# Dilated attention tiles ahead of the plain ones, and the first batch's low-rank product in fp32, in a fused attention and FFN kernel on Trainium2

## The chip, the core and the metric

The kernel runs on one core of one Trainium2 chip. A core has five engines that are named here as the profile names them: PE (TensorE, the matrix products; PEld is its weight load), DVE (VectorE), ACT (ScalarE), POOL (GpSimd) and SP (SyncE, which here does nothing but issue DMA transfers, one after the other). Each engine works through its own instructions in a fixed order and waits on semaphores for the others. The metric is the device time of one execution in microseconds (us).

## What is computed

```python
def _attn_ref(q, k, v):                       # 8 batches, 8 heads, S=576, D=64
    scores = scale * np.matmul(q, k.transpose(0, 1, 3, 2))
    rel = pos[:, None] - pos[None, :]
    mask_plain = (rel >= 0) & (rel < window)                     # window 32, heads 0 to 3
    mask_dil = (rel >= 0) & (rel < window * dilation) & (rel % dilation == 0)   # dilation 4, heads 4 to 7
    ...                                                          # masked softmax
    return np.matmul(attn, v)

def _moe_ref(x, U, V, w_ch1, w_ch2):          # x: 8 x 576 x 512 from the attention
    h = x.transpose(0, 2, 1) @ U @ V          # U: 576 x 32, V: 32 x 576, mixes along the sequence
    u = x + h.transpose(0, 2, 1)
    ch = np.maximum(u @ w_ch1, 0.0) @ w_ch2   # 512 -> 2048 -> 512
    return u + ch
```

## The kernel before

**Layout.** The 8 x 576 tokens are 36 tiles of 128 tokens, `x_tile(t)`, 512 wide: columns 0 to 255 hold the four plain heads (half 0), 256 to 511 the dilated ones (half 1). The FFN goes over 12 chunks of three tiles (384 tokens). In a chunk 16 blocks `f` run: `layer1(f)` (L760 on) makes `ph` out of `u` transposed and the columns of `w_ch1` (products at L771), ACT applies the relu (`hh`, L776), DVE makes the rest `hl` (L777), and `layer2(f)` adds three products per tile into `acc` (L791). FFN operands are split into a high and a low part in the type fp32r, with three products each: high times high, high times low, low times high.

**Attention.** A batch is nine groups `g` of two tiles of 64 queries (`TILES`, L49, sets which). Scores (L389 for the first two batches, in fp32), softmax (DVE L409, ACT L413), transposes of the weights (PE L426, copied as `pt` at L428 and L430), products with `v` (`weighted`, PE L452), and an eviction that divides by the sum (DVE L482, four operations per group). A plain tile is evicted straight into its rows of `x`. A dilated tile holds every fourth token, is evicted to `xp`, and SP then moves it row by row with DMAs `x<-xp` (L486) to where its tokens stand. Batch 0 is a prologue; batch 1 is laid over chunk 0, and every later batch over the chunks that follow.

**The mix.** `t` is U times x, per batch in two column halves, `t_0` (plain) and `t_1` (dilated). `split` (L494 on) splits a piece of x into `xhl` (ACT cast L500, subtraction L502), `t_mm` (L509 on) adds two fp32r products per piece (L522), and `t_evict` (L527 on) splits `t` once more into `ts` (ACT L531 and L537, DVE L532 and L534). `mix` adds V times t to x (PE `m`, L546, DVE L548). The three tiles of chunk 0 do it otherwise: `lay_x` (L556) transposes x by products with the identity, `lay_mix` (L563) adds the mix to the transposed tile, `transp` (L604, L605) splits that into `uth` and `utl`, and `add_mix` (L569) puts the mix into `acc`.

**Weights.** The two weight matrices arrive as 32 pieces of 64-bit words, `raw` (512 KB, SP L202 and L204). `weight_step` runs a pipeline over the pieces: ACT narrows in three operations (`narrow_a`, L211 to L213), DVE shifts (L219), POOL adds (L220), then the high part is a cast on ACT (L224) or DVE (L226) and the low part a subtraction on POOL or DVE (L227). Pieces alternate: `w1(f)`, `w2(f)`. All 32 are prepared between the end of the prologue and the end of chunk 0. The first three small pieces are U and V.

**What sets the order.** A scheduler of the framework turns the program into a fixed order per engine: by priorities, by the order in which the program issues, and by its own estimates. The program steers it with tables at its head: after which step of batch 0 a weight step stands (`PRE_AT`, `W_FROM`, `W_EACH`, `PRE_N`), and which engine takes a cast (`H_ON_ACT`, `XL_DVE`, `XL_LAST`). `batch_items` (L608 on) lists the pieces of a batch in order, with a place in time for each.

## Time and profile before

| | |
|---|---|
| median of three runs | 1012.73 us (1011.54 to 1014.42) |
| the profiled execution, time | 1013.52 us |
| its span | 1011.7 us |
| mean granted clock of PE | 0.982 |
| busy: PE, PEld, DVE, ACT, POOL | 984.7, 864.9, 626.8, 408.6, 328.3 us |
| chain that ended last, by engine | PE 89%, DVE 4%, DMA 2%, POOL 1%, ACT 1%, issue 1% |
| largest groups of PE | layer 2 `acc` (three groups, 576 each) 229.3, 228.0, 212.0 us; layer 1 `ph` (three groups, 768 each) 175.5, 174.3, 173.2 us |

The span is the time from the first to the last instruction that the profiler saw; the time of the execution has some us around it. The chain follows the work that ended last backwards, at each step to what released it. An engine's idle time means something only where the chain runs through it. SPq rows are SP's issues of transfers: the second number of such a row is how long the issues of that group took, not how long the transfers took.

### The profile page before, as it was taken

To read this page: it belongs to the slowest core of one execution; us is meant where nothing else is said; L and a number is where in the kernel's file an instruction comes from. 1 tells how busy PE (TensorE), PEld (TensorE's weight loads), DVE (VectorE), ACT (ScalarE), POOL (GpSimd) and SP (SyncE) were. 2 spreads that over 40 slices of the span, in tenths; PEclk is the share of its full clock that TensorE was granted. 3 is DMA by queue.
4 is the path that set the end of the run, shared out by engine and by line. 5 is a ranking of instruction groups with operands and counts; after the bars stand their busy time and mean duration, and the time that the engine had idled before them with its cause. 6 is when DMAs were issued, how large, how long until landed. Compare 5 with 4: busy or idle time off the path is not lost.

```text
span 1011.7 us, 18252 instructions
## 1 busy us (share of the span) xinstructions
PE 984.7 (97%) x5928; PEld 864.9 (85%) x5928; DVE 626.8 (62%) x2149; ACT 408.6 (40%) x985; POOL 328.3 (32%) x520
## 2 busy tenths in 40 slices
PE   7699999999999999999999999999999999999998
PEld 6598778888988889888888888788898888899996
DVE  4989877776468747777468763877647864311211
ACT  5799954343244424344244432434324432111110
POOL 0579954252133413153132431434222421000000
PEclk9789997999999999999999999999999999999999
DMA  9688634342333325243242332424232420400000
GB/s 291 186 276 270 183 120 110 81 129 85 75 88 112 86 59 140 77 120 83 66 124 73 114 83 73 122 77 124 85 88 80 119 64 22 135 1 1 32 1 32
DMA packets 96912, 103.34 MB, mean 102 GB/s; under 512 B 12816, under 2 KB 83536, under 8 KB 96816
## 3 DMA queue, kind: packets, MB, share of 16 engines
q1 hardware_dynamic: 96816, 102.16, 35.6%
q8 instruction: 48, 0.79, 0.3%
q14 instruction: 48, 0.39, 0.1%
...
## 4 chain that ended last, share of the span: by engine, by line
PE 89%; DVE 4%; DMA 2%; POOL 1%; ACT 1%; issue 1%; SPq 0%; DVEq 0%; POOLq 0%
PE ph L771 38%; PE acc L791 38%; PE pv L452 4%; PE s L378 3%; PE t L522 2%; PE s L389 1%; PE m L546 1%; DMA qk<-qk 1%; POOL v L220 1%; DMA v<-vv 1%; DVE v L219 0%; DVE w1h L226 0%; PE tp L556 0%; PE ptp L426 0%; DVE xp L482 0%
## 5 line engine op out<-in xcount | busy, mean ns | idle before, releaser
L791 PE MATMUL acc<-w2h,hh 128*128 128x512 f32 x576 | 229.3, 398 | 1.1 <-DVE x L816 1.1
L791 PE MATMUL acc<-w2l,hh 128*128 128x512 f32 x576 | 228.0, 396 | 0.0
L355 POOL TENSOR_TENSOR qks<-qkr,qks 128x160 fp32r<-128x160 f32 x192 | 103.2, 538 | 382.5 <-ACT qks L354 255.7
L777 DVE SCALAR_TENSOR_TENSOR hl<-ph,hh 128x384 fp32r<-128x384 f32 x192 | 106.1, 553 | 176.4 <-ACT hh L776 175.1
L791 PE MATMUL acc<-w2h,hl 128*128 128x512 f32 x576 | 212.0, 398 | 0.0
L776 ACT ACTIVATE hh<-ph 128x384 fp32r<-128x384 f32 x192 | 93.3, 486 | 268.7 <-PE ph L771 247.6
L771 PE MATMUL ph<-uth,w1l 128*128 128x384 f32 x768 | 175.5, 340 | 0.0
L771 PE MATMUL ph<-uth,w1h 128*128 128x384 f32 x768 | 174.3, 341 | 0.7 <-ACT uth L604 0.7
L771 PE MATMUL ph<-utl,w1h 128*128 128x384 f32 x768 | 173.2, 338 | 0.6 <-DVE utl L605 0.6
L413 ACT ACTIVATE p<-p,nmax 128x160 f32<-128x160 f32 (+1 forms) x288 | 110.7, 407 | 115.8 <-DVE nmax L409 114.8
L771 PEld LDWEIGHTS ph<-uth,w1h 128*128 128x128 f32 x768 | 139.1, 190 | 17.2 <-ACT uth L604 1.9
L771 PEld LDWEIGHTS ph<-uth,w1l 128*128 128x128 f32 x768 | 136.7, 189 | 1.1 <-issue 0.2
L771 PEld LDWEIGHTS ph<-utl,w1h 128*128 128x128 f32 x768 | 135.2, 188 | 2.4 <-DVE utl L605 1.0
L354 ACT CAST qks<-qkr 128x288 fp32r<-128x288 f32 x192 | 80.7, 429 | 125.2 <-PE s L378 92.0
L791 PEld LDWEIGHTS acc<-w2h,hl 128*128 128x128 f32 x576 | 107.2, 188 | 23.7 <-issue 0.2
L791 PEld LDWEIGHTS acc<-w2h,hh 128*128 128x128 f32 x576 | 108.2, 188 | 17.9 <-ACT hh L776 1.7
L791 PEld LDWEIGHTS acc<-w2l,hh 128*128 128x128 f32 x576 | 108.2, 188 | 15.9
L439 DVE STREAM_TRANSPOSE pt<-p 32x128 f32<-32x128 f32 x384 | 115.7, 301 | 8.9 <-ACT p L413 4.0
L406 DVE TENSOR_TENSOR p<-s,wide_sb 128x160 f32<-128x160 f32 x192 | 60.3, 318 | 76.0 <-PE s L378 74.6
L358 POOL TENSOR_TENSOR qks<-qkr,qks 64x128 fp32r<-64x128 f32 x192 | 90.4, 471 | 15.1
L502 POOL TENSOR_TENSOR xhl<-x,xhl 128x256 fp32r<-128x256 f32 (+1 forms) x68 | 49.7, 753 | 79.3 <-ACT xhl L500 47.6
L409 DVE CUSTOM_DVE_ANT_0 p<-s,p 128x160 f32<-128x160 f32 x192 | 60.2, 320 | 3.9
...
## 6 DMA issues: line engine op xcount, KB each, us to landing
...
```

The costliest lines, as they stand in the source:

```text
L354: nc.scalar.copy(out=t[:, 0:QK2], in_=raw)
L355: nc.gpsimd.tensor_tensor(out=t[:, QK2:], in0=raw[:, P:], in1=t[:, P:QK2].bitcast(F32), op=ALU.subtract)
L358: eng.tensor_tensor(out=t[lo, 0:P], in0=raw[lo, 0:P], in1=t[lo, 0:P].bitcast(F32), op=ALU.subtract)
L406: nc.vector.tensor_tensor(out=p_sb[:, u, :], in0=sp[:, 0:KW], in1=wide_sb[:, kind], op=ALU.add)
L409: nc.vector.tensor_tensor_reduce(out=p_sb[rs, u, 0:w], in0=a, in1=c, scale=-1.0 / 8.0, scalar=3.0e38, op0=ALU.add, op1=ALU.min, accum_out= ...
L413: nc.scalar.activation(out=p_sb[:, u, 0:w], in_=p_sb[:, u, 0:w], func=AF.Exp, bias=nmax[:, u:u + 1], scale=-1.0,)
L439: nc.vector.transpose(out=to[:, :, WIN * (r % 2):WIN * (r % 2 + 1)], in_=p_sb[rs, :, QB * s + WIN * k:QB * s + WIN * (k + 1)])
L502: eng.tensor_tensor(out=xl[rs], in0=x[rs], in1=xh[rs].bitcast(F32), op=ALU.subtract)
L771: nc.tensor.matmul(ph, lhsT=w[:, k, :], rhs=u[:, k, :], start=(n == 0), stop=(n == len(seq) - 1))
L776: nc.scalar.activation(out=hh, in_=ph, func=AF.Relu)
L777: nc.vector.scalar_tensor_tensor(out=hl, in0=ph, scalar=0.0, in1=hh.bitcast(F32), op0=ALU.max, op1=ALU.subtract)
L791: nc.tensor.matmul(acc[i], lhsT=h[:, ss], rhs=w, start=(c > 0 and f == 0 and n == 0), stop=(f == FC - 1 and n == 2))
```

## The change

All batches now take the dilated tiles first (groups 0 to 3, and one half of group 4) and the plain ones last. The products with `v` are laid so that a group of two dilated tiles, or of two neighbouring plain ones, stands in PSUM in the order of its target, and is evicted by one operation of 128 rows (others by two of 64). The `t` of batch 0 is made in fp32 out of `x` and `xp` themselves, with U in fp32, so that batch 0 has no `xhl`; the second row block of its `ts` is left at zero, cleared once by POOL. The dilated half `t_1` is summed and split while the plain tiles are still at work, and `lay_x` and `lay_mix` go by halves. In the later batches too the dilated half comes first. Three weight steps follow the items 8 to 10 of batch 0, and five more are issued behind the last split of `t`. For the first six weight pieces the high part is cast on ACT throughout (three of them were on DVE).

The core of the diff:

```diff
-TILES = [(0, j) for j in range(NJ)] + [(1, NJ - 1)] + [(1, j) for j in range(NJ - 1)]
+TILES = [(1, j) for j in range(NJ)] + [(0, NJ - 1)] + [(0, j) for j in range(NJ - 1)]
-PRE_AT = range(5, 11)
+PRE_AT = range(3, 9)
-W_FROM = 11
-W_EACH = 3
+W_AT = range(8, 11)
-XL_LAST = 3
-XL_DVE = ((0, 1), (1, 1))
+H_FIRST = 9
+XL_DVE = ((1, 0),)
-XPS = 4
+XPS = 5
+    t0s = [const.tile([P, HALF_D], F32R, name=f"t0_{c}") for c in range(2)]
+    for e in t0s:
+        nc.gpsimd.memset(e[2 * RANK:3 * RANK].bitcast(F32), 0.0)
...
-                for dst, src in ((us, v3[:, 0:9]), (held_u[0], v3[:, 9:])):
-                    nc.scalar.copy(out=dst[:, :, 0:RANK], in_=src)
-                    nc.vector.tensor_tensor(out=dst[:, :, RANK:], in0=src, in1=dst[:, :, 0:RANK].bitcast(F32), op=ALU.subtract)
+                nc.scalar.copy(out=us[:, :, 0:RANK], in_=v3[:, 0:9])
+                nc.vector.tensor_tensor(out=us[:, :, RANK:], in0=v3[:, 0:9], in1=us[:, :, 0:RANK].bitcast(F32), op=ALU.subtract)
...
-            narrow_c(v, h, l, nc.vector if n % L_ON_DVE == 0 and n >= L_FROM else nc.gpsimd, n % 4 < H_ON_ACT)
+            narrow_c(v, h, l, nc.vector if n % L_ON_DVE == 0 and n >= L_FROM else nc.gpsimd, n % 4 < H_ON_ACT or n < H_FIRST)
...
-        for u in range(UNITS):
-            v_sb = loaded[g, 1, u // 2]
+        tiles = [tile_of(g, 2 * i) for i in range(2)]
+        rows = [row_of(b, *e) for e in tiles]
+        for u in range(2):
             for h in range(2):
                 hs = slice(h * DV, (h + 1) * DV)
-                nc.tensor.matmul(pv[QB * h:QB * (h + 1), u, :], lhsT=pt[:, u, QB * h:QB * (h + 1)],
-                                 rhs=v_sb[:, u % 2, hs], start=True, stop=True)
+                for i in range(2):
+                    last_pv[g] = nc.tensor.matmul(pv[rows[i]:rows[i] + QB, 2 * u + h, :], lhsT=pt[:, 2 * i + u, QB * h:QB * (h + 1)],
+                                     rhs=loaded[g, 1, i][:, u, hs], start=True, stop=True)
...
-            dst4 = dst.rearrange("p (u h d) -> p u h d", u=2, h=2)
-            for h in range(2):
-                rs = slice(QB * h, QB * (h + 1))
-                nc.vector.tensor_tensor(
-                    out=dst4[:, :, h, :], in0=pv[rs, us_, 0:D],
-                    in1=ssum[rs, us_].unsqueeze(2).broadcast_to([QB, 2, D]), op=ALU.mult)
+        if parts[0][2] == parts[1][2] and (parts[0][2] == 1 or rows == [0, QB]):
+            parts = [(parts[0][0], 0, 2)]
+        for dst, row, both in parts:
+            rs = slice(row, P if both == 2 else row + QB)
+            nc.vector.tensor_tensor(
+                out=dst[rs].rearrange("p (e d) -> p e d", d=D), in0=pv[rs, :, 0:D],
+                in1=ssum[rs].unsqueeze(2).broadcast_to([rs.stop - rs.start, UNITS, D]), op=ALU.mult)
...
-            split(b, part, 1, xp, slice(0, QB * len(DPART[part])))
+            xps[part] = xp
...
+    def t_first(i, c):
+        if c == 0:
+            t, row, n, tok = batch_parts(0)[i]
+            rs = slice(row, row + n)
+            k = 8 if n < P else tok // P
+            m = x_tile(t)[:, 0:HALF_D]
+        else:
+            rs = slice(QB * (2 - len(DPART[i])), P)
+            k = 9 + i
+            m = xps.pop(i)
...
+        nc.tensor.matmul(t_ps[0, c], lhsT=held_u[0][rs, k * RANK:(k + 2) * RANK], rhs=m[rs],
+                         start=new, stop=(i == (0 if c else len(DPART) - 2)))
...
-        if b == 0:
-            nc.vector.tensor_copy(out=ts_[r[2]], in_=tp[r[1]])
-        else:
+        if b > 0:
             nc.scalar.copy(out=ts_[r[2]], in_=tp[r[1]])
-        nc.scalar.copy(out=ts_[r[3]], in_=tp[r[0]])
+        held_t[:] = [nc.scalar.copy(out=ts_[r[3]], in_=tp[r[0]]), low]
...
+    def first_of(g):
+        if g <= ODD:
+            t_first((g + 1) % len(DPART), 1)
+        if g == ODD:
+            t_evict(0, 1)
+        if g >= ODD:
+            t_first((g - ODD - 1) % len(DPART), 0)
...
-        for c in range(2):
+        for c in (1, 0):
...
-    for _ in range(PRE_N):
-        weight_step(NSMALL, NPIECE)
+    with tc.issue_after(held_t[0].ins), tc.issue_after(held_t[1].ins):
+        for _ in range(PRE_N):
+            weight_step(NSMALL, NPIECE)
```

What this makes of the order is shown at three places. In the rows, a name like `raw_492` is a buffer with its number; line numbers are those of the program the rows are from (after the change lines stand 6 to 36 further down).

**SP, at the end of batch 0's loads.** Before, three loads for batch 1's scores and three for its `v`, then the first two weight fetches (`raw_500`, `raw_502`), three moves, and the next fetch:

```order
L337 DMA qkr_780<-qk 128x448
L337 DMA qkr_782<-qk 128x448
L337 DMA qkr_784<-qk 128x448
L319 DMA v_0_837<-vv 96x260
L319 DMA v_1_839<-vv 96x260
L319 DMA v_0_911<-vv 96x260
L202 DMA raw_500<-w 128x4x256
L204 DMA raw_502<-w 128x1024
L486 DMA x_260<-xp_341 16x256
L486 DMA x_298<-xp_341 32x256
L486 DMA x_338<-xp_341 16x256
L202 DMA raw_545<-w 128x4x256
```

Now two `qkr` loads are followed by 24 moves, of which the last three stand here, and the weight fetches come behind these and four loads:

```order
L497 DMA x_195<-xp_368 16x256
L497 DMA x_197<-xp_368 32x256
L497 DMA x_239<-xp_368 16x256
L345 DMA qkr_646<-qk 128x448
L327 DMA v_0_699<-vv 96x260
L327 DMA v_1_701<-vv 96x260
L327 DMA v_0_773<-vv 96x260
L208 DMA raw_492<-w 128x4x256
L210 DMA raw_494<-w 128x1024
L208 DMA raw_523<-w 128x4x256
L210 DMA raw_554<-w 128x1024
```

The weight fetches moved behind all moves of batch 0.

**ACT, around the split of `t`.** Before, four weight pieces are narrowed ahead of the first `t_0` cast (their last two steps, and the cast of the first high parts, stand here):

```order
L224 CAST w2h_86<-v_580 128x512
L212 ACTIVATE sign_76<-raw_584 128x512
L213 ACTIVATE sign_76<-raw_584 128x512
L500 CAST xhl_4_1_570<-xp_559 128x256
L531 CAST ts_0_602<-t_0_573 32x256
L224 CAST w1h_84<-v_596 128x4x128
L537 CAST ts_0_602<-t_0_573 32x256
L531 CAST ts_1_663<-t_1_607 32x256
L537 CAST ts_1_663<-t_1_607 32x256
L211 ACTIVATE v_630<-raw_600 128x512
```

Now the split of `t_1` stands before any weight, and that of `t_0` between the narrowing of the first two pieces (`t_1_78` and `t_0_77` are the split halves, `t_1_395` and `t_0_446` the sums in PSUM):

```order
L552 CAST t_1_78<-t_1_395 32x256
L251 CAST vs<-v_404 128x352
L556 CAST t_1_78<-t_1_395 32x256
L217 ACTIVATE v_519<-raw_492 128x512
L218 ACTIVATE sign_75<-raw_492 128x512
L219 ACTIVATE sign_75<-raw_492 128x512
L552 CAST t_0_77<-t_0_446 32x256
L217 ACTIVATE v_550<-raw_494 128x512
L218 ACTIVATE sign_76<-raw_494 128x512
L219 ACTIVATE sign_76<-raw_494 128x512
L556 CAST t_0_77<-t_0_446 32x256
L217 ACTIVATE v_596<-raw_523 128x512
```

The casts of `xhl` are gone, `t_1`'s split moved ahead of the weights, and each half of `t_0`'s split stands behind one narrowing.

**DVE, at the end of chunk 0.** Before, the three final adds (L816) and then the mix adds (L548) of batch 1's second half, all five behind `hl_15`:

```order
L777 SCALAR_TENSOR_TENSOR hl_15_1984<-ph_15_1946,hh_15_1983 128x384
L816 TENSOR_TENSOR x_184<-acc_0_798,x_184 128x512
L816 TENSOR_TENSOR x_222<-acc_1_799,x_222 128x512
L816 TENSOR_TENSOR x_260<-acc_2_800,x_260 128x512
L548 TENSOR_TENSOR x_338<-x_338,m_0_1_1732 64x256
L548 TENSOR_TENSOR x_927<-x_927,m_1_1_1744 128x256
L548 TENSOR_TENSOR x_985<-x_985,m_2_1_1755 128x256
L548 TENSOR_TENSOR x_1040<-x_1040,m_3_1_1764 128x256
L576 STREAM_TRANSPOSE z_2674<-x_985 128x4x4x32
L548 TENSOR_TENSOR x_1092<-x_1092,m_4_1_1770 128x256
```

Now three of them stand ahead of the final adds:

```order
L813 SCALAR_TENSOR_TENSOR hl_15_1894<-ph_15_1856,hh_15_1893 128x384
L567 TENSOR_TENSOR x_239<-x_239,m_0_0_1642 64x256
L567 TENSOR_TENSOR x_789<-x_789,m_1_0_1654 128x256
L567 TENSOR_TENSOR x_791<-x_791,m_2_0_1665 128x256
L852 TENSOR_TENSOR x_191<-acc_0_660,x_191 128x512
L852 TENSOR_TENSOR x_193<-acc_1_661,x_193 128x512
L852 TENSOR_TENSOR x_195<-acc_2_662,x_195 128x512
L567 TENSOR_TENSOR x_794<-x_794,m_3_0_1674 128x256
L594 STREAM_TRANSPOSE z_2595<-x_791 128x4x4x32
L567 TENSOR_TENSOR x_796<-x_796,m_4_0_1680 128x256
```

The half that comes last in a batch is now the plain one, and three of its five adds moved ahead of the chunk's final adds.

## Rows read from the trace of the kernel before

**Rows 1.** From the page: the span in 40 equal slices of 25.3 us; each digit is the clock that PE was granted, in tenths of full speed.

```profile
PEclk9789997999999999999999999999999999999999
```

**Rows 2.** The waits of PE from 300 to 1012 us: line that waited, what released it, us in total, times, longest.

```profile
PE acc L791 <- DVE x L816: 1.1, 1, 1.1
PE ph L771 <- ACT uth L604: 0.7, 2, 0.4
PE ph L771 <- DVE utl L605: 0.6, 1, 0.6
```

**Rows 3.** Busy time by window: length of the window, then PE, PEld, DVE, ACT and POOL busy in us with the number of instructions, PE's granted clock, the DMA share and GB/s.

```profile
40.00:45.00 5.00, 1.78 (x8) 1.00 (x7) 4.88 (x10) 3.21 (x6) 3.67 (x5) 0.50 0.15 36
...
60.00:80.00 20.00, 20.00 (x141) 17.81 (x140) 17.84 (x54) 19.34 (x42) 19.27 (x15) 1.00 0.84 266
```

**Rows 4.** The waits of PE from 25 to 56 us, columns as in rows 2.

```profile
PE pv L452 <- DVE pt L430: 4.0, 1, 4.0
PE t L522 <- DVE xhl L502: 3.2, 2, 2.2
```

**Rows 5.** The waits of PE from 56 to 140 us, columns as in rows 2.

```profile
PE m L546 <- ACT ts L537: 0.7, 1, 0.7
PE pv L452 <- DMA v<-vv: 0.5, 1, 0.5
PE t L522 <- POOL xhl L502: 0.3, 1, 0.3
PE pv L452 <- DVE pt L430: 0.2, 1, 0.2
```

**Rows 6.** DVE in order of time, in batch 0: start, us, line, operation, out<-in with shapes, how many in a row. First an eviction of a group, then one mix add.

```profile
14.01 1.19 DVE L482 TENSOR_TENSOR x<-pv,ssum 64x128 f32<-64x128 f32 x4
...
50.60 0.42 DVE L548 TENSOR_TENSOR x<-x,m 128x256 f32<-128x256 f32 x1
```

**Rows 7.** The chain of waits from 26 to 29 us: start, us, engine, tile, line, instructions.

```profile
27.39 0.47 PE tp L556 x4
```

**Rows 8.** SP's queue in order of time, columns as in rows 6.

```profile
26.48 0.40 SPq L202 DMA_DIRECT2D raw<-w  x1
27.46 0.36 SPq L204 DMA_DIRECT2D raw<-w  x1
28.21 2.64 SPq L486 DMA_DIRECT2D x<-xp  x3
...
33.17 13.18 SPq L486 DMA_DIRECT2D x<-xp  x21
```

**Rows 9.** All weight fetches issued at L202 (`w1` pieces): from issue to landing.

```profile
DMA to landing us min/median/max: 3.1/4.9/6.3
```

**Rows 10.** ACT in order of time, columns as in rows 6; in brackets how long it sat idle before, and what ended that.

```profile
33.56 0.66 ACT L211 ACTIVATE v<-raw 128x512 f32<-128x512 f32 x1
34.12 0.77 ACT L212 ACTIVATE sign<-raw 128x512 f16<-128x512 f32 x1
...
35.36 0.64 ACT L211 ACTIVATE v<-raw 128x512 f32<-128x512 f32 x1
...
41.05 0.60 ACT L224 CAST w2h<-v 128x512 fp32r<-128x512 f32 x1
41.55 0.79 ACT L212 ACTIVATE sign<-raw 128x512 f16<-128x512 f32 x1
...
45.87 0.36 ACT L531 CAST ts<-t 32x256 fp32r<-32x256 f32 x1 [2.66 <-PE t L522]
...
52.82 1.53 ACT L604 CAST uth<-tp 128x512 fp32r<-128x512 f32 x3
...
57.87 1.16 ACT L413 ACTIVATE p<-p,nmax 128x96 f32<-128x96 f32 x4
...
60.64 0.49 ACT L776 ACTIVATE hh<-ph 128x384 fp32r<-128x384 f32 x1 [0.48 <-PE ph L771]
```

**Rows 11.** PE in order of time, at the mix of batch 0.

```profile
48.38 1.11 PE L563 MATMUL tp<-vs,ts 128*128 128x128 f32 x4
...
52.36 0.95 PE L546 MATMUL m<-ts,vs 128*128 128x256 f32 x3
```

**Rows 12.** The chain of waits from 53 to 64 us, columns as in rows 7.

```profile
53.40 2.88 PE s L389 x12
56.28 0.48 PE acc L569 x2
56.76 2.91 PE ph L771 x16
...
62.39 1.40 PE acc L791 x6
```

**Rows 13.** POOL in order of time: the low part of `w1(3)`.

```profile
64.42 1.29 POOL L227 TENSOR_TENSOR w1l<-v,w1h 128x512 fp32r<-128x512 f32 x1
```

**Rows 14.** PE in order of time: the first products of block 3 with that low part.

```profile
71.37 0.86 PE L771 MATMUL ph<-uth,w1l 128*128 128x384 f32 x4
```

**Rows 15.** All high parts of `w1` cast on DVE (L226): durations in ns, least, middle and longest, and first and last start.

```profile
L226 DVE CAST w1h<-v x8: 425/1456/1525, 39.1 to 128.0; 128x512 fp32r<-128x512 f32 x8
```

**Rows 16.** DVE in order of time, at the end of chunk 0.

```profile
148.62 1.89 DVE L816 TENSOR_TENSOR x<-acc,x 128x512 f32<-128x512 f32 x3 [2.66 <-PE acc L791]
150.53 1.54 DVE L548 TENSOR_TENSOR x<-x,m 64x256 f32<-64x256 f32 x4
```

119 lines of the change are left out of this document (64 added, 55 removed).

## The prediction, made before the changed kernel ran

> **What bounds the kernel now.** I read the page first: a span of 1011.7 us, and the granted clock of PE (TensorE), at full speed but for three slices early on [rows 1]. The profiled execution took 1013.5 us; the median of the three runs, 1012.7, stands 0.8 lower, so I sum against 1013.5 and take 0.8 off at the end. Then the waits of PE by stretch. After 300 us PE waits 2.4 us in all [rows 2]: there PE sets the time, and an edit that only spares another engine is worth nothing. Between 25 and 56 us lies the one real hole. PE is busy 1.78 of the 5 us from 40 to 45, at the lower of its two clock levels (0.50) [rows 3]; it waits for a copy of `pt` (4.0 us) and for the low parts `xhl` of batch 0 (3.2 us) [rows 4]. From 60 to 80 us (chunk 0, the first 384 tokens of the FFN, with batch 1's attention and all the weight work beside it) PE is busy 20 of 20 us, but so nearly are ACT (19.3) and POOL (19.3) [rows 3]: chunk 0 belongs to PE with little room on the others. Its waits by name come to 1.7 us [rows 5].
>
> **Prologue, what goes.** Batch 0's ten high-part casts on ACT, ten subtractions, and half the `t` products disappear, and with them the wait for `xhl`. Four evictions of 64x128, 1.19 us a group on DVE, become one of 128x256. No such eviction is in the trace; its nearest row of that shape is the mix add, 0.42 us [rows 6], so about 0.77 us of DVE per group is spared, at worst nothing (if reading PSUM with a broadcast factor costs what the four did). Until about 25 us the scores wait for their loads, and I count nothing there.
>
> **Ten fp32 products in place of 20 split ones.** The nearest fp32 row with 128 partitions is `lay_x`, four of 128 columns in 0.47 us at full clock [rows 7], so 0.24 us for 256 columns and 0.47 at half clock. Ten at 0.47 are 4.7 us, at 0.24 2.4 us. They stand in a stretch where PE waits anyway; if that cover were gone, only the last one of `t_0` would be on the path. I count 0, bounds 0 and +0.5.
>
> **Prologue, the new gate.** The dilated tiles now come first, so their 24 moves (`x<-xp`) stand together on SP's queue. Before, only three of them stood behind the first two weight fetches, which were issued at 26.48 and 27.46, and 21 went from 33.17 to 46.35, 0.63 us each; none can be issued before its tile is evicted [rows 8]. Now 24 moves, one `qkr` and three `v` loads precede the first weight fetch `raw_492`. The first six moves fall into the slots that a `qkr`, three `v` loads and two fetches had (to about 28.0; each issue there waits for a transfer eight places ahead of it to land, so I keep the pace). Eighteen more at 0.60 give 38.8, four short issues at about 0.4 give 40.2: `raw_492` leaves **13.7 us later** than its counterpart. Landing took 3.1 to 6.3 us, median 4.9, mostly on a loaded DMA [rows 9]; now little else moves, so I take 4.0: 44.2, bounds 43.3 and 46.5.
>
> This would be hidden, if the order on ACT did not put `t_0`'s split **behind** it: the narrowing of `raw_492` to fp32, then the first `t_0` cast, then that of `raw_494`, then the second. So `t` does not run ahead of the weights as the program's text suggests. A narrowing is three ACT operations; from the start of one at 33.56 to the next at 35.36 are 1.80 us, 0.56 of them the first; a `t` cast takes 0.36 [rows 10]. From 44.2: 1.80 + 0.36 + 1.80 + 0.36 = 48.5. PE's last `t_0` product is done by about 42 by the same rows and is not the gate. Six `lay_mix` products of `c=0` at 0.25, 1.5 us, three `m` at 0.3, 0.9 us [rows 11], twelve scores 2.88 and the first `add_mix` 0.48 [rows 12] give 54.3 for the first product of layer 1, against 56.76: **-2.4 us**.
>
> **How much of that ACT lets through.** ACT has been idle since about 34, has no narrowing done (before, four by 43), and takes over three weight casts. In its order, from the second `t_0` cast to the first relu `hh_0`, stand five first steps of a narrowing at 0.56, four second and third steps at 1.24, four casts at 0.5 (start to start), three casts `uth` 1.53 and four exponentials 1.17 [rows 10]: 2.8 + 5.0 + 2.0 + 1.5 + 1.2 = 12.5 us without a gap. So `hh_0` starts at 61.0 (before 60.64), and layer 2's first product at 61.4 against 62.39 [rows 12]. Only **-1.0 us** of the 2.4 is kept, bounds -1.9 and +1.3 by the landing.
>
> **Chunk 0 beyond that.** PE has the same products there. Weights are some 4 us behind: low part `w1l(3)` was begun on POOL at 64.42 and done at 65.7, and PE used it at 71.37 [rows 13, 14], 5.7 us later. With 4 us less, and PE 1.0 us earlier, 0.7 us remains: tight, but no wait. POOL and ACT leave some 7 us between 60 and 140, so the weights catch up near the middle of the chunk. Of the 1.7 us of named waits [rows 5] those for `ts` (a cast that was late), and for POOL's `xhl`, could go: I take **-1.0**, bounds 0 and -1.7.
>
> For the three moved casts the row of DVE's own casts has 0.43 us at least, 1.46 in the middle [rows 15]; I reckon 3 x 0.43 = 1.3 us of DVE spared, and ACT pays 3 x 0.5. The long ones lie beside POOL's operations. The Trainium skill (SBUF — State Buffer, Who interferes with whom) says that a cast can take the port pair that DVE shares with GpSimd for its whole length, so that the other stands still; the spread in the trace agrees. By that rule the casts would free 3 x 1.46 = 4.4 us of DVE and part of POOL, and the tight places above would hold. By the row alone they are as tight as told.
>
> **End of chunk 0.** Before, all five mix adds of batch 1's second half follow the three final adds on DVE (1.89 us), the first four in 1.54 us, 0.38 each [rows 16], and PE's transposes for chunk 1 wait for them. Now three of five stand ahead of the final adds, beside layer 2's last products: 3 x 0.38 = **-1.1 us**, bounds 0 and -1.5.
>
> **Later chunks.** Order of the halves, moves and evictions change, PE's work does not; of the 2.4 us of waits left after 300 us [rows 2] I count 0, bounds +-0.5.
>
> Sum: -1.0 - 1.0 - 1.1 = -3.1, so 1010.4 for a profiled execution and **1009.6** for the median; its own range is 1007.5 to 1012.
>
> **Rivals.** *The gate opens early.* If transfers land sooner once the big loads are fewer, the first moves leave from 22 us on and `raw_492` some 2.5 us earlier. `t_0`'s products at about 42 then gate; ACT's row of 12.5 us starts at 46, and the whole 2.4 and more is kept: -3.5 - 1.0 - 1.1, about 1007. For it: the DMA is nearly idle then; against it: moves depend on landings and on evictions.
>
> *ACT eats the start.* If ACT or DVE push a few more casts ahead of the relus in the first four blocks, both prologue and wait terms vanish and only the boundary stays: about 1011.6. For it: ACT is busy 19.3 of 20 us [rows 3].
>
> *Slower: the late weights stop PE.* This decides from `raw_492` landing at about 46 or the weights being over 5.7 us behind at `w1l(3)`. Each further microsecond is then one that PE waits, in blocks 3 to 7; at 3 to 4 us late, with +1.3 at the start, -1.1 at the end and nothing of the waits, it gives +3 to +4: about 1016.5. For it: all weights begin 13.7 us later and POOL and ACT have 7 us of room; against it: before, ACT lay idle too, 2.7 us ahead of its first `ts` cast alone [rows 10], so the real lag is smaller.
>
> *The change does not do what it says*: weight steps stand ahead of `t_0`'s split on ACT, not behind. That is in the forecast.
>
> **Numbers.** A measurement of this kernel tells about 0.3%, 3.0 us, from no change: faster means below 1009.7, slower above 1015.8. Forecast 0.44, half of it on either side of 1009.7; early gate 0.20, faster; ACT eats it 0.18, same; late weights 0.18, slower. So faster 0.42, same 0.40, slower 0.18. The range leaves out the best of the early gate (three moves more in free slots) and the worst of the late weights: 1004.5 to 1016.0.
>
> **What would show it.** On SP 24 moves in a row and the first weight fetch at about 40; on ACT an idle stretch from about 34 to 44, then narrowing, `t_0`, narrowing, `t_0`; first layer-1 product near 54.3, `hh_0` near 61.0; no PE wait for `w1l` or `w2l` above 1 us in chunk 0; PE's gap behind the chunk's last product shorter by about 1 us; equal chunks after that. It is wrong if `raw_492` is issued before 36 or after 43, if PE waits several microseconds for weights, or if chunks 1 to 11 change by over 1 us.

## The result: slower, and the profile after

The changed kernel takes **1019.74 us** (median of 6 runs, 1017.83 to 1021.59) against 1013.58 (6 runs, 1011.27 to 1016.72) on the same chip: a ratio of **1.0060, interval 1.0042 to 1.0077**. Forecast was 1009.6, range 1004.5 to 1016.0. The profiled execution took 1018.54 us, its span is 1016.7.

I cut both spans at four marks that can be found in any of these traces: the first product of layer 1, the last relu of chunk 0 (`hh_15`), the first product of layer 1 in chunk 1, and the end.

| us | before | after | difference |
|---|---|---|---|
| start to first layer-1 product | 56.55 | 58.61 | +2.1 |
| chunk 0, to `hh_15` | 88.3 | 94.6 | +6.3 |
| `hh_15` to chunk 1's first product | 13.6 | 14.2 | +0.6 |
| the rest | 853.3 | 849.4 | -3.9 |

A relu is marked at its start. These lengths come from one execution each, and executions of one kernel spread by up to 8.5 us (e6 below), so a stage's length is read beside the mean clock that PE was granted in it: in chunk 0 1.00 before and 0.99 after, from `hh_15` on to chunk 1 (the boundary) 0.78 and 0.72.

**The fetch.** SP's queue after, columns as in [rows 8]:

```profile
24.22 17.69 SPq L497 DMA_DIRECT2D x<-xp  x24
41.95 0.58 SPq L345 DMA_DIRECT2D qkr<-qk  x1
42.58 1.37 SPq L327 DMA_DIRECT2D v<-vv  x3
43.99 0.43 SPq L208 DMA_DIRECT2D raw<-w  x1
```

All 24 moves ahead of the first weight fetch, as told; it leaves at 43.99 where its counterpart left at 26.48 [rows 8].

**ACT**, columns as in [rows 10]:

```profile
48.64 0.66 ACT L217 ACTIVATE v<-raw 128x512 f32<-128x512 f32 x1 [14.06 <-DMA raw<-w]
...
50.45 0.34 ACT L552 CAST t<-t 32x256 fp32r<-32x256 f32 x1
50.70 0.66 ACT L217 ACTIVATE v<-raw 128x512 f32<-128x512 f32 x1
...
52.67 0.36 ACT L556 CAST t<-t 32x256 fp32r<-32x256 f32 x1
...
65.53 0.46 ACT L812 ACTIVATE hh<-ph 128x384 fp32r<-128x384 f32 x1
```

The reader sees the gate of the prediction: ACT idles 14.06 us, then narrowing, `t_0`, narrowing, `t_0`, then work without a gap to `hh_0`, 12.5 us after 53.05. The order held; it stands 4.5 us late.

**PE** waits for that gate. Its waits from 25 to 56 us, then its rows:

```profile
PE tp L582 <- ACT t L556: 6.5, 1, 6.5
PE tp L576 <- DMA x<-xp: 2.2, 2, 1.7
```

```profile
53.08 1.54 PE L582 MATMUL tp<-vs,t 128*128 128x128 f32 x6 [6.46 <-ACT t L556]
...
58.61 1.48 PE L807 MATMUL ph<-uth,w1h 128*128 128x384 f32 x4
...
77.35 0.94 PE L807 MATMUL ph<-uth,w1l 128*128 128x384 f32 x4
...
159.20 0.47 PE L386 MATMUL s<-qks 128*128 128x320 f32 x1 [1.71 <-DVE x L567]
...
165.59 1.09 PE L618 MATMUL tp<-id_sb,x 128*128 128x128 f32 x4 [2.25 <-DVE utl L624]
...
167.35 1.65 PE L807 MATMUL ph<-uth,w1h 128*128 128x384 f32 x4
```

**Chunk 0.** The windows of [rows 3], and POOL's low part `w1l(3)`, which answers to [rows 13]:

```profile
40.00:45.00 5.00, 4.49 (x18) 3.24 (x17) 0.00 (x0) 0.00 (x0) 0.00 (x0) 0.50 0.36 98
60.00:80.00 20.00, 19.11 (x137) 16.79 (x136) 13.57 (x44) 20.00 (x44) 17.44 (x14) 0.99 0.83 245
```

```profile
72.95 1.48 POOL L233 TENSOR_TENSOR w1l<-v,w1h 128x512 fp32r<-128x512 f32 x1
```

From 60 to 80 us ACT is full (20.00 of 20), POOL is less busy than before, and PE has lost 0.9 us. The low part is done at 74.43 and used at 77.35: 2.9 us of lead, where before there were 5.7. Later it shrinks to almost nothing: worked out for blocks 9 to 14, 0.1 to 0.8 us (before, 4.4 to 10.0). The whole of chunk 0, before and then after, in the same columns:

```profile
56.55:144.87 88.32, 86.74 (x589) 75.00 (x589) 76.80 (x204) 77.81 (x178) 77.15 (x61) 1.00 0.70 213
```

```profile
58.61:153.19 94.58, 91.24 (x594) 77.15 (x594) 72.72 (x183) 84.10 (x189) 79.63 (x66) 0.99 0.67 211
```

PE's idle time inside chunk 0 is 3.3 us (94.58 less 91.24), before 1.6. The other 4.5 us stand as busy time, five more products among them: the records of neighbouring products overlap (one of 512 columns lasts 0.39 us and the next starts 0.23 us after it began), so a product that starts a little late leaves no gap. The named waits of PE from 56 to 150 us, the longest three, and the one wait of a weight load (PEld) for a low part `w1l`:

```profile
PE acc L827 <- ACT hh L812: 0.9, 1, 0.9
PE pv L465 <- DVE pt L438: 0.8, 1, 0.8
PE t L543 <- DVE xhl L512: 0.7, 1, 0.7
...
PEld ph L807 <- POOL w1l L233: 0.4, 1, 0.4
```

So the leads are tight, but PE hardly waits for a low part; it waits for the relu `hh_0`, a copy `pt` and a part `xhl`.

**The boundary.** DVE after, where [rows 16] stood:

```profile
155.82 1.21 DVE L567 TENSOR_TENSOR x<-x,m 64x256 f32<-64x256 f32 x3 [1.54 <-PE m L565]
156.94 1.88 DVE L852 TENSOR_TENSOR x<-acc,x 128x512 f32<-128x512 f32 x3
...
163.92 0.71 DVE L594 STREAM_TRANSPOSE z<-x 128x512 f32<-128x512 f32 x1 [0.68 <-DMA zd<-z]
...
164.77 0.68 DVE L624 TENSOR_TENSOR utl<-tp,uth 128x512 fp32r<-128x512 f32 x1
```

Three mix adds did move ahead of the final adds. But a later transpose `z` waits on DVE for a buffer that a DMA still reads, the split `utl` of chunk 1 is queued behind it, and PE waits 2.25 us for `utl`.

**Later chunks.** PE's windows from 620 to 650 us, before and then after:

```profile
620.00:650.00 30.00, 27.90 (x154) 24.20 (x153) 19.93 (x63) 11.36 (x27) 10.60 (x20) 1.00 0.51 134
```

```profile
620.00:650.00 30.00, 30.00 (x155) 27.27 (x154) 19.49 (x59) 10.96 (x26) 8.42 (x16) 1.00 0.47 126
```

The waits of [rows 2] are gone: after 300 us no wait of PE is named. The prediction counted them at 0; they are part of the -3.9.

### The profile page after: what moved, and what is told of

It is laid out like the page before. It is cut to its first block, busy times and chain, and to the rows that moved or that the text cites. A ratio compares the mean times of both kernels' runs of the same rounds, so it can differ in the third digit from the quotient of the medians.

```text
span 1016.7 us, 18019 instructions
## 1 busy us (share of the span) xinstructions
PE 988.2 (97%) x5928; PEld 866.5 (85%) x5928; DVE 578.0 (57%) x1944; ACT 405.6 (40%) x977; POOL 323.8 (32%) x520
## 4 chain that ended last, share of the span: by engine, by line
PE 83%; DVE 0%; DMA 0%; DVEq 0%; ACT 0%; issue 0%; SPq 0%
PE ph L807 37%; PE acc L827 37%; PE pv L465 3%; PE s L386 3%; PE t L543 2%; PE m L565 1%; PE s L397 1%; DMA zd<-z 0%; DVE x L852 0%; PE tp L618 0%; DVE z L594 0%; DVE utl L624 0%; DVEq L929 0%; ACT uth L623 0%; SPq L351 0%
## 5 line engine op out<-in xcount | busy, mean ns | idle before, releaser
L807 PE MATMUL ph<-utl,w1h 128*128 128x384 f32 x768 | 177.2, 340 | 0.0
L807 PE MATMUL ph<-uth,w1l 128*128 128x384 f32 x768 | 172.0, 340 | 0.1
L807 PE MATMUL ph<-uth,w1h 128*128 128x384 f32 x768 | 171.8, 341 | 0.1
L827 PEld LDWEIGHTS acc<-w2l,hh 128*128 128x128 f32 x576 | 108.2, 188 | 16.9 <-POOL w2l L233 0.3
L366 POOL TENSOR_TENSOR qks<-qkr,qks 64x128 fp32r<-64x128 f32 x192 | 89.2, 465 | 15.0
```

What stands on the lines that cost most here:

```text
L366: eng.tensor_tensor(out=t[lo, 0:P], in0=raw[lo, 0:P], in1=t[lo, 0:P].bitcast(F32), op=ALU.subtract)
L807: nc.tensor.matmul(ph, lhsT=w[:, k, :], rhs=u[:, k, :], start=(n == 0), stop=(n == len(seq) - 1))
L827: nc.tensor.matmul(acc[i], lhsT=h[:, ss], rhs=w, start=(c > 0 and f == 0 and n == 0), stop=(f == FC - 1 and n == 2))
```

## The experiments

Five batches of runs, each with its own runs of the kernel before (medians 1013.3 to 1014.4); every ratio is to those. Kernels whose profiled spans differ by under 1 us from that of the changed one (e3, e4) stand 0.0024 to 0.0031 below it in another batch, so between batches I read little into less than 0.003. "Lead" is the time from the end of a low part `w1l` to its first use on PE, worked out from the trace.

### First round: the changed kernel, one thing at a time

**e1_fetch_early**: two weight pieces fetched after item 5, ahead of the moves.

```diff
-RAWS = 4
+RAWS = 5
+        if i == FETCH_AT:                      # 5
+            sent[NSMALL] = [NSMALL, NSMALL + 1]
+            for n in sent[NSMALL]:
+                pipe[n] = fetch64(n)
```

> The changed kernel, but the first two weight fetches stand ahead of the 24 moves on SP's queue, with one more buffer for them. Theory (the first fetch leaves 17.5 us later than before, and ACT, which narrows the weights ahead of all else, has a row of 12.5 us from there to the first relu): both fetches leave near 21 us and land near 30; t_0's split follows PE's last t_0 product at about 47; first layer-1 product at 53 to 54 (58.6 in the changed kernel), first relu at 58 to 59 (65.5), the end of chunk 0 earlier by 6 to 9 us; time 1011 to 1014. Rival (the weights are not what is late; chunk 0 is slower because its order of small products is finer): the first relu comes sooner, but chunk 0 keeps its 4 us, time 1015 to 1018. Rival (the moves, not the fetches, gate): no gain over 1.5 us, since the moves leave later by what the fetches take.

Measured 1017.58, ratio 1.0032 [1.0022, 1.0043]. The first fetch left at 20.6, first layer-1 product 54.56, `hh_0` 60.2: the start that was forecast. But the third fetch still left at 45.0, chunk 0 took 98.0 us (granted clock 0.94 there), and the time hardly moved.

**e2_split_first** (`W_AT = ()`, `PRE_N = 8`): all narrowings behind `t_0`'s split.

> The changed kernel, but every weight step stands behind t_0's split, so that ACT splits t_0 ahead of the first narrowing; the fetches stay behind the moves. Theory (landing of the first fetch at 48.6 and ACT's full row from there count): t_0's split ends at about 47.5, but by its order ACT still has 14.4 us of work from 48.6 to the first relu, so that comes at about 63 (65.5), and the time falls by 1 to 3 us. Rival (the place of t_0's split behind two narrowings is the cost): first layer-1 product 5 us sooner and the time 5 us less.

1020.21, 1.0051 [1.0032, 1.0070]: `hh_0` 63.2, but chunk 0 101.2. The earlier start is paid back: the first low part of `w1` is done at 57.2 us (55.6 in the changed kernel), and here PE does wait for weights in chunk 0, 1.8 us for `w1l` and 2.3 us for `w1h`.

**e3_raws5** (`RAWS` 4 to 5 alone):

> The changed kernel with five instead of four buffers for raw weights and nothing else: what the extra buffer of the run with early fetches does alone. Theory: the first fetch leaves at 44 as before, later fetches a little sooner; time within 1.5 us of the changed kernel. Rival (fetches inside chunk 0 run short of buffers, and this starves ACT): 3 us or more are gained in chunk 0.

1017.17, 1.0029 [1.0016, 1.0042]; chunk 0 92.4, the boundary 15.1.

**e4_z3** (`ZS` 2 to 3, a third buffer for `z`):

> The changed kernel with three instead of two buffers z for transposing tiles on DVE. Theory (at the end of chunk 0 the third transposition waits for a transfer out of z, and the low part utl that PE needs stands behind it on DVE): the wait of 2.2 us of PE on utl near 163 us goes, time 1.5 to 2.5 us less than the changed kernel. Rival (something else is late by then, the mix adds or nmax): under 0.7 us.

1017.81, 1.0036 [1.0022, 1.0049]. Boundary 13.4 in place of 14.2: the buffer is worth 0.8 us of the boundary. PE's wait for `utl` fell from 2.2 to 1.1 us and did not go, and a wait of 0.9 us for `nmax` took part of its place.

**e5_casts_dve** (`H_FIRST` 9 to 0, the three casts back on DVE):

> The changed kernel with three casts of weight high parts back on DVE (H_FIRST 0). Theory A (ACT has no gap from the landing of the first fetch to the first relu, so each cast there counts): two casts fewer in that row, first relu 1.0 us earlier (64.5 in place of 65.5), time 1 to 2 us less. Rival (a long DVE cast beside POOL holds up both, so the weights' low parts come later): the time is the same or up to 2 us more.

1016.24, **1.0010 [0.9989, 1.0031]**: by the ratios 0.5% better than the changed kernel, the largest step of this round, but that is between batches, where e3 and e4 too stand 0.2 to 0.3% better. The profiled spans differ by 0.7 us alone (1016.0 and 1016.7; this execution took 1.6 us more than the median). `hh_0` came 0.7 us earlier (64.82). Chunk 0 (95.0, granted clock 0.96) did not shorten; the boundary did, 14.2 to 11.3, with a granted clock of 0.88 against 0.72.

**e6_four_early**: four weight pieces fetched after item 3 and narrowed from item 6.

```diff
-PRE_N = 5
-W_AT = range(8, 11)
+PRE_N = 3
+W_AT = range(6, 11)
+        if i == FETCH_AT:                      # 3
+            ...
+            sent[NSMALL] = list(range(NSMALL, NSMALL + 4))
+            for n in sent[NSMALL]:
+                pipe[n] = fetch64(n)
```

> The changed kernel with the first four weight pieces fetched near 20 to 30 us (two ahead of the moves, two among them; the three small raw buffers stand in the early pool for that) and narrowed on ACT ahead of t_0's split. Theory W (weights' preparation lags by a third of its whole length because ACT stood idle for 14 us, and the lag paces chunk 0: low parts of w1 were done 0 to 1 us ahead of their product in blocks 9 to 14): low part of w1(3) done by about 66 (74.4), five us or more ahead of its product, chunk 0 from first product to last relu 89 to 91 us (94.6; before 88.3), time 1008 to 1012. Rival S (in chunk 0 batch 1's moves now stand among the weight fetches on SP's queue, and delay these and PE's loads): chunk 0 still takes 94 us or more, time 1015 or more.

1016.36, 1.0027 [1.0008, 1.0046]. Leads of 6 to 22 us, so weights are not late at all, and yet chunk 0 takes 99.5 us. The profiled execution took 1021.93 us, the longest of ten, and PE's granted clock in its chunk 0 was 0.93, so part of the 99.5 is its own. PE's waits from 56 to 150 us:

```profile
PE s L400 <- DMA qkr<-qk: 1.5, 1, 1.5
PE pv L468 <- DVE pt L441: 1.5, 1, 1.5
PE pv L468 <- DMA v<-vv: 1.4, 1, 1.4
```

These two loads landed late: the `qkr` 8.0 us after its issue at 99.64, the `v` 5.4 us after its issue at 120.70, each issued right behind two or three weight fetches. So "late weights" is not the whole cause.

**e7_b1_plain_first**: batch 1 back to plain tiles first (`order_of(b)`, its `c` order, its `XL_DVE`).

> The changed kernel, but batch 1 alone takes its plain tiles first again (and its plain half of t first); all else, the late first fetch too, as in the changed kernel. Rival S (batch 1's moves among the weight fetches): moves stand at the end of chunk 0 as before, chunk 0 shortens by 3 us or more, time 1013 to 1015. Theory W (weights that began late): chunk 0 keeps 93 us or more, the same time as the changed kernel within 1.5 us. The end of chunk 0 also shows whether its wait on DVE's transposition comes from the order of the halves.

1021.02, 1.0070 [1.0053, 1.0086]: no gain by itself.

### Second round: parts of the change put into the kernel before

**e8_before_late_order**: the kernel before, dilated first only from batch 2 on.

```diff
+OTHER = [(1, j) for j in range(NJ)] + [(0, NJ - 1)] + [(0, j) for j in range(NJ - 1)]
+def order_of(b):
+    return TILES if b < SPLIT else OTHER       # SPLIT = 2
-        for c in range(2):
+        for c in range(2) if b < SPLIT else (1, 0):
```

> The kernel before, with dilated tiles first and the dilated half of t first in batches 2 to 7 alone: prologue and chunk 0 as before. Theory (chunks 1 to 11 of the changed kernel win 3 us since PE's waits at the ends of chunks 5 and 8, 2.6 and 0.5 us, are gone with the new order of the halves): those waits go, time 2 to 3.5 us less than before. Rival (these waits differ by the phase in which chunk 1 begins): the waits stay and the time is that of before within 1 us.

**1008.80, 0.9951 [0.9936, 0.9965].** Start and chunk 0 as before (56.3, 89.0), the rest 847.4 in place of 853.3. This part gains 5 us.

**e9_early_b1_plain** (e6 and e7 together):

> The changed kernel with both repairs: the first four weight pieces fetched and narrowed early (as in the run with four early) and batch 1 with its plain tiles first (as in that run). Theory (two causes, each enough to slow chunk 0: weights that start late, and batch 1's 24 moves among weight fetches and loads on SP's one queue): chunk 0 takes 88 to 91 us from its first product to its last relu, time 1008 to 1011. Rival (what slows chunk 0 is elsewhere in the change: whole evictions and the order of products with v, or casts on ACT): chunk 0 stays at 94 us or more, time 1014 or more.

1016.26, 1.0017 [1.0001, 1.0034]: it missed, and the rival's range came true. Leads 6 to 17 us, chunk 0 94.9 (granted clock 0.97). Something else in the change slows chunk 0.

**e10_before_b1_too** (e8 with batch 1 dilated first as well):

> The kernel before with dilated tiles first in batches 1 to 7 (in the run with the late order alone: 2 to 7, 1008.8 us); prologue and weight fetches as before. Theory S (batch 1's moves among the weight fetches in chunk 0): chunk 0 grows from 89.0 us to 92 or more, with waits of PE on loads (qkr, v) or on late low parts, time 1011 to 1014. Rival (only late weights matter): chunk 0 stays at 88 to 90 us, time 1007 to 1010.

1010.73, 0.9961 [0.9941, 0.9980]: chunk 0 92.1, the boundary 11.0 in place of 13.6. From `hh_0` to `hh_15` it takes 86.8 us, e8 84.2; the boundary gives that back, at a granted clock of 1.00 where e8 has 0.82. In sum batch 1's order costs 0 to 2 us, no more than two batches can tell apart.

**e11_before_late_fetch**: the kernel before, every weight step behind batch 0's last move.

```diff
-    for _ in range(PRE_N):
-        weight_step(NSMALL, NPIECE)
+    with tc.issue_after(last_move[0].ins):
+        for _ in range(PRE_N + len(early_steps)):
+            weight_step(NSMALL, NPIECE)
```

> The kernel before with all weight fetches behind the last move of batch 0, nothing else. Theory W (late weights): first fetch near 47 us (26.5 before), first layer-1 product at 59 to 61 (56.6), low parts of w1 at most 2 us ahead of their products in most blocks, chunk 0 of 92 us or more (88.3), time 1018 to 1022. Rival (the weights catch up beside PE): the start is lost, 3 to 4 us, and chunk 0 keeps its 88 to 89 us, time 1016 to 1017.

1026.95, **1.0126 [1.0106, 1.0146]**. SP's queue there:

```profile
27.89 16.67 SPq L488 DMA_DIRECT2D x<-xp  x24
44.61 0.58 SPq L202 DMA_DIRECT2D raw<-w  x1
```

The fetch leaves within 0.6 us of that of the changed kernel, chunk 0 takes 101.4 us (granted clock 0.93), leads are 0.1 to 3 us but for the last block. Late weights are enough, alone, to make this kernel 12.6 us slower; but they are later here than in the change (first narrowing at 50.64 us, there 48.64; second fetch at 48.10, there 44.52).

**e12_late_order_whole**: e8 with the change's whole evictions and its order of the products with `v`.

> The run with the late order alone (the kernel before with dilated tiles first in batches 2 to 7, 1008.8 us) plus the changed kernel's whole evictions and its order of products with v. Theory (DVE's evictions are hidden behind PE): DVE spends about 0.75 us less per group, time within 1.5 us of 1008.8. Rival (the new order of products with v or the two-part evictions disturb chunk 0): 2 us or more slower, chunk 0 over 91 us.

**1006.82, 0.9928 [0.9904, 0.9952]**, faster than both kernels. First layer-1 product 52.63 (before 56.55), chunk 0 90.6. Its leads are 0.1 to 4.0 us from block 2 on: short leads alone do not make chunk 0 long.

### Third round: what else slows chunk 0

**e13_moves_pool**: the changed kernel, batch 0's moves issued by POOL.

```diff
-            nc.sync.dma_start(out=x_tile(t)[to:...], in_=xp[r:r + n])
+            (nc.gpsimd if b == 0 else nc.sync).dma_start(out=x_tile(t)[to:...], in_=xp[r:r + n])
```

> The changed kernel, with one word changed: batch 0's 24 moves x<-xp are issued by POOL and not by SP; loads and weight fetches stay on SP, in the same order, and so no longer stand behind the moves. Theory (one issue queue: the weights AND batch 1's qkr and v loads wait for the moves, whichever stands behind the other, and all that the change lost is that): raw_492 leaves at 27 to 31, the loads before it at 24 to 28, first layer-1 product 50 to 54, hh_0 at 57 to 60, chunk 0 at most 91.5 us, the time 1006.5 to 1010, so faster than before. Rival (fp32 t, the casts on ACT and the order of batch 0 itself slow chunk 0): weights and loads early, chunk 0 still 94 us or more, the time 1014 or more. Second rival: POOL is slow to issue moves or the issues hold its arithmetic up: the last move lands later than 43 and the first layer-1 product comes after 56.

1015.76, **1.0014 [0.9999, 1.0029]**, by the ratios 4.6 us better than the changed kernel; the profiled spans differ by 4.7 us (1012.0 and 1016.7). SP and then ACT:

```profile
28.47 0.40 SPq L208 DMA_DIRECT2D raw<-w  x1
```

```profile
43.31 0.36 ACT L552 CAST t<-t 32x256 fp32r<-32x256 f32 x1 [5.97 <-PE t L532]
...
47.82 1.20 ACT L217 ACTIVATE v<-raw 128x512 f32<-128x512 f32 x2
...
60.22 0.47 ACT L812 ACTIVATE hh<-ph 128x384 fp32r<-128x384 f32 x1
```

The queue was the gate of the start: the fetch leaves 15.5 us earlier, and `hh_0` comes 5.3 us earlier. The theory that the queue explains all fell, and the first rival's range came true: chunk 0 still takes 94.5 us. Its leads are those of the changed kernel, 0.1 to 0.8 us in blocks 10 to 14, since PE starts earlier by as much as the weights do.

**e14_four_on_act** (the first four fetches issued by ACT, moves on SP):

> The changed kernel with the first four weight pieces fetched early, as in e6_four_early, but issued by ACT (from about 24 us) instead of SP; the moves and then qkr and v stay on SP as in the changed kernel. Theory (one queue): the weights are early and the moves are not displaced (last at about 42), but the qkr and v loads still leave at 42 to 44: first layer-1 product 53 to 56, low parts of the weights 5 us or more ahead, chunk 0 between 91 and 96 with waits for qkr and v, the time 1010 to 1014. Rival (weights alone): chunk 0 at most 91 and the time 1007 to 1009. Rival (order of batch 0 itself): 1015 or more.

1017.30, 1.0026 [1.0013, 1.0038]; first layer-1 product 60.3, chunk 0 95.2. The time is in the range of the last rival (the order of batch 0), but the start came 4 to 7 us later than the first theory had it, so the three are not told apart.

**e15_moves_act** (the 24 moves issued by ACT):

> The changed kernel with batch 0's 24 moves issued by ACT. SP is as free as in e13_moves_pool, but each move costs ACT's sequencer time between exponentials, so scores and t come later. Theory (one queue): raw_492 leaves at 27 to 31, first layer-1 product 52 to 56, chunk 0 at most 92, the time 1008 to 1012. Rival (order of batch 0 itself): chunk 0 at 94 or more, the time 1014 or more.

1029.15, 1.0147 [1.0132, 1.0162]: first layer-1 product at 68.8. ACT's exponentials wait behind its issues (ten of them took 10.64 us, from 24.05 on); a bad remedy, and no test of chunk 0.

**e16_pool_weights_early** (e9 with moves on POOL):

> e9_early_b1_plain (weights fetched and narrowed ahead of t's split, batch 1 with the plain tiles first) with batch 0's 24 moves issued by POOL, as in e13_moves_pool. In e13 the first fetch left at 28.5 and hh_0 came at 60.2, but the third narrowing still waited for t's split until 47.8, the low parts were as tight as in the changed kernel and chunk 0 took 94.5 us. Theory (narrowing behind t's split is the second half of the loss; early weights must not come at the price of late loads or moves): hh_0 at 58 to 62, low parts 4 us or more ahead, chunk 0 at most 92 us, the time 1006 to 1010, faster than before. Rival (casts on ACT, fp32 t or batch 0's order slow chunk 0): chunk 0 at 94 or more, 1013 or more.

1017.80, 1.0037 [1.0018, 1.0056], chunk 0 95.5. The edit did not do its work: ACT's order still put the second steps of the first narrowings behind `t_0`'s split (50.33 us), and the first `w1l` was begun at 55.49 us (e13: 50.09). It says nothing on early weights.

**e17_narrow_behind_t**: e12 with its fetches where they are, every narrowing behind `t`'s split.

```diff
+    with tc.issue_after(held_t[0, 0].ins), tc.issue_after(held_t[0, 1].ins):
+        for _ in range(PRE_N + len(early_steps)):
             weight_step(NSMALL, NPIECE)
```

> e12_late_order_whole, whose batch 0 is that of the kernel before, with the weight fetches where they are, but every narrowing of a weight behind batch 0's split of t. Theory (narrowing behind t's split costs by itself): first narrowing at 47 to 50 and not 33, low parts under 3 us ahead, hh_0 later by 2 to 5, chunk 0 at 94 or more, the time 1006.8 + 6 to 12 = 1013 to 1019. Rival (only the late fetch costs, since the pieces lie ready): within 2 us of e12, 1005 to 1009.

1008.09, 0.9945 [0.9929, 0.9962]: 1.7 us by the ratios, 3.5 between the profiled executions (1008.79 and 1005.28): nearer to the rival's answer. ACT:

```profile
43.18 0.67 ACT L222 ACTIVATE v<-raw 128x512 f32<-128x512 f32 x1
...
60.82 0.50 ACT L796 ACTIVATE hh<-ph 128x384 fp32r<-128x384 f32 x1
```

The first narrowing is 10 us later than [rows 10] had it, `hh_0` comes 3.3 us later than in e12, chunk 0 is 92.6. Narrowing late is cheap beside e11's 12.6 us, as long as the pieces lie ready.

**e18_casts_act**: e12 with the casts of the first six weight pieces on ACT.

```diff
-            narrow_c(v, h, l, ..., n % 4 < H_ON_ACT)
+            narrow_c(v, h, l, ..., n % 4 < H_ON_ACT or n < 9)
```

> e12_late_order_whole with the first casts of the weights (pieces below 9, three more than before) on ACT and not DVE, as in the changed kernel. Theory (late weights are all that chunk 0 lost): within 2 us of e12, 1005 to 1009, chunk 0 between 90 and 92. Rival (the casts on ACT make ACT late for hh): hh_0 1 us or more later, chunk 0 at 93 or more, the time 1009 to 1012.

1013.91, **0.9999 [0.9981, 1.0016]** against 0.9928: **7 us for three casts by the ratios, 5.0 between the profiled executions** (1010.31, the shortest of ten, and 1005.28), and `hh_0` 1.6 us later: the rival, with a larger loss than it had. Windows of e12, then of e18:

```profile
52.00:72.00 20.00, 20.00 (x145) 18.01 (x145) 14.70 (x49) 20.00 (x43) 18.22 (x14) 1.00 0.93 308
```

```profile
52.00:72.00 20.00, 18.35 (x133) 16.57 (x132) 12.89 (x46) 20.00 (x43) 16.89 (x14) 1.00 0.88 290
...
125.00:130.00 5.00, 3.87 (x12) 3.22 (x13) 1.90 (x5) 4.94 (x15) 4.84 (x6) 0.72 0.56 165
```

ACT has 20.00 of 20 us either way. The casts take 1.8 us off DVE, where there was room, and ACT can't do more; POOL, which is fed by ACT, falls by 1.3 us (its adds wait 8.3 us for ACT there, 5.5 in e12) and PE by 1.65. How PE comes to wait stands on DVE in e18:

```profile
57.54 1.03 DVE L230 TENSOR_SCALAR v<-v 128x512 int32<-128x512 int32 x1 [2.35 <-ACT v L222]
58.49 0.67 DVE L441 COPY pt<-ptp 96x512 f32<-96x512 f32 x1
...
148.97 1.88 DVE L828 TENSOR_TENSOR x<-acc,x 128x512 f32<-128x512 f32 x3
...
156.04 0.71 DVE L588 STREAM_TRANSPOSE z<-x 128x512 f32<-128x512 f32 x1 [0.76 <-DMA zd<-z]
156.68 0.65 DVE L617 TENSOR_TENSOR utl<-tp,uth 128x512 fp32r<-128x512 f32 x1
```

and on PE:

```profile
59.22 0.69 PE L466 MATMUL pv<-v,pt 96*64 96x65 f32 x16 [1.25 <-DVE pt L441]
...
126.13 0.50 PE L803 MATMUL acc<-w2h,hh 128*128 128x512 f32 x1 [2.12 <-ACT hh L788]
...
127.60 0.63 PE L803 MATMUL acc<-w2l,hh 128*128 128x512 f32 x1
...
157.48 1.08 PE L611 MATMUL tp<-id_sb,x 128*128 128x128 f32 x4 [2.10 <-DVE utl L617]
```

DVE sits idle 2.35 us for a narrowing step of ACT, and the copy `pt` behind it makes PE wait 1.25 us. A relu near 126 us comes 2.12 us late; none of the moved casts stands near it (the first six high parts are cast by 61 us), so that is the changed order and not their time. And the boundary takes 15.0 us in place of 11.5. DVE there, in e12:

```profile
146.53 0.71 DVE L588 STREAM_TRANSPOSE z<-x 128x512 f32<-128x512 f32 x1
147.17 1.89 DVE L828 TENSOR_TENSOR x<-acc,x 128x512 f32<-128x512 f32 x3
```

In e12 the scheduler put the first `z` ahead of the final adds (`acc`); in e18 (rows from 148.97 on) every `z` comes behind them, the buffer wait of a later one falls on `utl`, and PE waits 2.10 us. That is the pattern of the changed kernel's boundary, brought about by moving three casts: the fixed order of ACT's and DVE's rows differs in dozens of places between the two programs. The boundary's window in e12, then in e18, in the columns of [rows 3]:

```profile
143.28:154.73 11.45, 7.71 (x39) 5.74 (x39) 9.35 (x25) 4.85 (x11) 3.56 (x8) 1.00 0.50 142
```

```profile
144.22:159.23 15.01, 10.49 (x41) 7.50 (x39) 10.12 (x29) 6.00 (x15) 3.90 (x8) 0.73 0.45 126
```

PE is idle 4.5 us there in place of 3.7, so waits are 0.8 of the 3.6 us; the rest is in products, which ran at a granted clock of 0.73 in place of 1.00. Over chunk 0 and the boundary together e18 takes 5.4 us more, 2.5 of them idle time of PE. Of its +1.9 in chunk 0 all lies ahead of `hh_0`: from there to `hh_15` e18 takes 85.1 us and e12 85.8.

## Why the prediction was wrong, step by step

**The sum.** Forecast was -1.0 for the start, -1.0 for chunk 0, -1.1 for its end and 0 for the rest: -3.1. The two traces, cut at `hh_0`, `hh_15` and chunk 1's first product, show +4.9, +3.4, +0.6 and -3.9: +5.0. The start failed by the queue, which e13 shows; chunk 0 failed too, and why is open in part.

**What the parts of the change come to.** In differences of the ratios: late order -0.49% (e8), whole evictions -0.23% (e12 to e8), casts on ACT +0.71% (e18 to e12) or +0.50% (after to e5), narrowing behind `t`'s split +0.17% (e17 to e12), fetches behind the moves +0.46% (after to e13): together **+0.4 to +0.6%**, measured +0.60%. All but the first are differences between batches, each with some 0.2 to 0.3% of its own, so it is partly luck that they meet. Five such terms leave about 0.5%, 5 us (an estimate: the root of the sum of their squares), for fp32 `t` and the other orders of batches 0 and 1, which no run takes by themselves.

**First fetch, 40.2 forecast, 43.99 measured: the step that failed first.** I gave the first six moves free slots up to 28.0 and 0.60 us to each other one. The moves began at 24.22; the first six were out at 29.7 (1.7 us later than told), the other eighteen took 12.2 us and not 10.8, waits for `xp` and for landings among them, and one `qkr` and three `v` issues took 2.0 us and not 1.4. Landing took 4.6, not 4.0. So ACT's start was 48.64 and not 44.2. It landed 2.6 us past the point that I had named for the rival of late weights (46).

**From there to `hh_0` the mechanism was right.** The order on ACT, its row of 12.5 us, the waits of PE for `t_0`: 65.53 is 48.64 plus 16.9, and the prediction added 16.8 to 44.2. The start then costs 4.9 us at `hh_0`, where I had 0.4 (61.0 against 60.64). With the queue freed (e13) `hh_0` comes at 60.22 and 4.7 of the 5.0 us go. One reading beside it was wrong without harm: PE's last `t_0` product was done at 46.6 and not by 42, still ahead of the first `t_0` cast at 50.45.

**Casts: mis-sized, and the sign with it.** I priced "3 x 0.43 us of DVE spared, ACT pays 3 x 0.5" into the row of ACT and counted nothing beyond. ACT was busy 19.34 of 20 us [rows 3]: the row said that ACT had no room, and I used it to support a rival and not in this term. Measured: 5.0 us between the profiled executions of e12 and e18 and 7 by the ratios; e5 the other way round 5 by the ratios, but 0.7 between the profiled spans. Most of e18's 5.0 is the boundary (+3.6), where the order changed and the granted clock was lower; so it is the price of the move with all that the scheduler made of it, and not of three casts as such. By the Trainium skill (SBUF — State Buffer, Who interferes with whom) a cast on DVE can hold the port pair that it shares with GpSimd for its whole length while the other stands still. By that rule both DVE and POOL should have gained by the move. The trace shows DVE's load fall (12.89 against 14.70 in e18), but not POOL's gain: it was fed less, and its busy time fell from 18.22 to 16.89.

**Chunk 0, -1.0 forecast, +3.4 from `hh_0` to `hh_15` measured; open in part.** "Tight, but no wait" nearly held for the low parts, though the weights never caught up: leads of 0.1 to 0.8 us in blocks 9 to 14, and one wait of 0.4 us for `w1l`. What failed is the -1.0: the waits that I let go were replaced by others, for `pt` and `xhl`, and by delays too short for a named wait. Late weights can act through a full ACT (84.10 us busy in chunk 0, before 77.81), but no run separates that. The moved casts do not explain it, for e18 takes no longer than e12 from `hh_0` to `hh_15`, and e5, with the casts back, takes 89.2 against 87.7 (its granted clock in chunk 0 was 0.96, though). Batch 1's order could (e10 takes 2.6 us more there than e8), but with batch 1 back in the old order the changed kernel takes 91.2 (e7).

**Boundary, -1.1 forecast, +0.6 measured.** The three adds moved as told, but what ended PE's last long wait was `utl` behind `z`. I had asked what is spared and not what is late next. The granted clock counts here too: the boundary takes 11.0 to 11.5 us in the three traces where it is 1.00 (e9, e10, e12), and 13.4 to 15.1 in ten where it is 0.72 to 0.82 (before, after, e8 and e18 among them); in the other seven, 10.4 to 13.2 at 0.72 to 0.91, the two go less closely together.

**Evictions, 0 forecast, -2.3 us (e12 to e8, two batches, so not certain by the times).** The profiled spans differ by 2.8 us, and the start bears it out: the first layer-1 product comes 3.7 us earlier with them (56.30 to 52.63), with PE's waits from 25 to 56 us falling from 3.1 to 0.9 for `pt` and from 3.2 to 2.2 for `xhl`. I had called the prologue's DVE time covered; there the copies `pt` and the parts `xhl` gated PE [rows 4], and both are DVE's.

**Later chunks, 0 forecast, -3.9 (e8: -5.9).** [Rows 2] named waits of 2.4 us, and I took them for a fixed cost of the kernel. They belonged to the order of the halves, and went with it (e8). They are less than half of e8's 5.9: PE's idle time there falls by 2.8 us, and no wait names the rest.

**The rivals.** *Late weights stop PE* is the one that came nearest (1016.5 against 1019.7, and I gave it 0.18). Its point of decision was passed on both counts: ACT began at 48.6, past 46, and `w1l(3)` was done 8.7 us later than before, not 5.7. Its mechanism, PE waiting a microsecond for each one in blocks 3 to 7, is not what the trace shows, so the near number is partly luck: 4.9 us were lost ahead of `hh_0`, where it had 1.3. *The gate opens early* fell at the queue. *ACT eats the start* named the right engine for a smaller loss.

**What stays open.** No run takes the changed kernel to the 1007 us of e12: e16 was to do it and did not do what it was meant to. What lengthens chunk 0 behind `hh_0` is not shown. What batch 0's own order with fp32 `t` costs or gains was not measured. And in several traces (e1 to e3, e5 to e7, e9, e11, e14 to e16) PE's granted clock in chunk 0 was 0.93 to 0.97, so their lengths of chunk 0 hold waits and clock together.
